# First routing: operands in the ranks' PSUM bank, first one-hots on ScalarE, the leading expert chosen right behind the ranks

## The chip, the cores and the metric

One core of a Trainium2 chip runs the whole kernel. The metric is the device time of one execution in microseconds (us), lower is better. The time before is 495.26 us, the median of 3 runs (494.83 to 495.79).

## What is computed

A linear attention with a normalised output is followed by two mixtures of experts (8 experts, 512 wide, 1024 hidden), each of which sends a token to one expert:

```python
kv = np.einsum('bhsd,bhse->bhde', k, v)
out = np.einsum('bhsd,bhde->bhse', q, kv)           # 4 x 8 x 576 x 64
rms = np.sqrt(np.mean(out * out, axis=-1, keepdims=True) + 1e-06)
x = (out / rms * g_norm)                             # as 2304 tokens x 512
# first mixture: tokens with x @ w_skip > 0 only
e_idx = np.argmax(xc @ w_gate, axis=1)
h = np.maximum(xc[mask] @ w1[e], 0.0)
y[mask] = gate_w[mask, None] * (h @ w2[e]);  out[do_compute] = xc + y
# second mixture: all tokens, at most `capacity` per expert, output gate_w * y
```

## The kernel before

The 2304 tokens are 18 tiles of 128. Tiles 0 to 8 are the first half of the first routing, 9 to 17 the second half (they are routed apart, so that the first half's work begins while attention still runs).

Attention goes batch by batch. `emit_kv` sums the key-value product of the next batch on TensorE (PE) in the PSUM bank `acc`. `emit_kvT` then transposes it into the bank `lg`, and two ScalarE (ACT) copies bring it to the SBUF matrix `kvbd`, which every product of that batch needs. `emit_products` computes one tile's output into `ops` (three buffers of two banks), and `emit_tile` normalises it: ACT squares (`sq`) and copies (`og`), VectorE (DVE) sums (`ss`), takes the reciprocal (`ri`), scales the logits (`lh`) and reduces them into `Lall`; GpSimd (POOL) does the two multiplications of 128 x 512 (`og`, `xr`), and a DMA in SyncE's queue (SP) writes the rows to the DRAM tensor `xcat`. `p1u` is a PSUM pool with a single bank each for the names `lg` and `acc`: a new tile of one name waits until all readers of the former are done.

The first routing of one half has these steps. `onehot_all` (L145) takes the maximum of the 8 logits per token, compares, weighs by expert number, takes the maximum again and compares, which gives the one-hot `oh`. `rank_part` (L167) scans it along the tiles (`C`, L173), lets PE add up ranks in `lg` (L178 to L183), and on DVE turns a rank into a block number `hb` and a row `a` within the block (L200 to L204). The tables are built from `os` and `Bt` (L207, L214) and from nine one-hots `As` of 128 x 128, one per tile (L218). Table matmuls (`As` against `Bt`, L794 and L855) then give for each expert's slots the token that sits in it.

The expert with the most tokens in the first half is the leader: `early1` (L780) counts the tokens in another tile `lg` and calls `lead` (L525), and `slot_reg` loads its number into a register, with which SP loads its weights (L329). `early1_rows` (L790) runs the table matmuls for it, makes the indices `gi` (L271 to L273) and gathers its first 128 rows. The expert runs on them in `EARLY_SEQ`: `t` transposes the rows, `h0` to `h3` are blocks of layer 1, `y0` to `y3` of layer 2, `R` the ranks of the second half, `T` the tables of all tokens, `v` dummy matmuls. Behind `T` DVE sorts the tables by slot, and it counts tokens that found no slot (`nrest`, L319). All engines load that count and branch on it (L372 to L374), and then the remaining experts run.

The order on PE is written out by hand: `ATT_SEQ` has a string for each batch (`t` a tile, `m` its products alone, `p` its rest, `c` a piece of the next batch's key-value product, `T` its transposes, `r` one-hots and scan, `R` ranks, `e` choice of the leader, `E` its table and gather, `w` a weight load). On the other engines a scheduler orders by priorities and dependencies; `behind` adds an order without a wait. `late` (L774) puts the first half's routing at the lowest priority.

Of the kernel before, what the change touches and what calls it, by code (L numbers as in the profile page):

```python
# [47 lines left out]
def moe_kernel(ctx: ExitStack, tc: tile.TileContext, qT, kk, vv, aux, w1a, w2a, w1b, w2b, capacity, out):  # L48
# [118 lines left out]
    def rank_part(st, ohv, i0, i1, ps_pool, tag, base=None, bump=None):  # L167
# [11 lines left out]
        if prev is not None:
            nc.tensor.matmul(R, lhsT=ones, rhs=prev.unsqueeze(2).to_broadcast([128, E, n]), start=False, stop=False)  # L180
        if bump is not None:
            nc.tensor.matmul(R, lhsT=identb, rhs=bump.unsqueeze(2).to_broadcast([128, E, n]), start=False, stop=False)
# [1 line left out]
        if prev is None:
            st["sum"] = C[:, :, n - 1]
        else:
            st["sum"] = rt.tile([128, E], BF16, name=nm("sum"))
            ins = nc.gpsimd.tensor_tensor(out=st["sum"], in0=prev, in1=C[:, :, n - 1], op=ALU.add)
            if m == 1 and bump is not None:
                behind(ins, ahead["gather"])  # L190
        if i1 == NT and m == 1:
            order_experts(st, ps_pool, tag)
# [1231 lines left out]
```

## Time and profile before

| what | us |
|---|---|
| median of the runs (3) | 495.26 |
| lowest, highest | 494.83, 495.79 |
| the profiled execution, its own time | 496.99 |
| its span, first to last instruction | 495.3 |
| TensorE matmuls busy in it | 472.4 (95%) |
| VectorE, ScalarE, GpSimd busy | 303.6, 205.3, 146.5 |

The profile is of one execution, and all times inside it are counted from the start of its span; the kernel's time is 1.69 us more than the span. In a timeline a row is a group of equal instructions that follow one another: the start, the time from the first's start to the last's end, engine, line, operation, output and inputs by the program's names, and the number of instructions. In brackets stand the engine's idle time just before and what ended it. Instructions of one engine overlap by about 0.1 us, so that a row may start before the last one ends.

### The profile page before, as it was taken

How to read it: one execution, taken by the hardware profiler on the slowest of the kernel's cores; microseconds unless marked ns; L12 is line 12 of the kernel's file. 1: busy time of each engine (PE TensorE's matmuls, PEld its weight loads, DVE VectorE, ACT ScalarE, POOL GpSimd, SP SyncE). 2: the span in 40 equal slices, each digit the busy share in tenths (PEclk: the TensorE clock that was granted, in tenths of full speed). 3: DMA queues.
4: the chain of work that ended last, by engine and by line, in shares of the span. 5: the costliest groups of instructions: out<-in, count | busy, mean ns of one | idle time of the engine just before them, and what ended most of it. 6: DMA issues, size and time to landing. Idle time of an engine off the chain costs nothing.

```text
span 495.3 us, 10229 instructions
## 1 busy us (share of the span) xinstructions
PE 472.4 (95%) x3829; PEld 450.1 (91%) x3829; DVE 303.6 (61%) x942; ACT 205.3 (41%) x524; POOL 146.5 (30%) x179
## 2 busy tenths in 40 slices
PE   6998689999999999999998999999999999999995
PEld 3897578999999999999897899999999999999984
DVE  2157988568766775356774576565657566675711
ACT  1376451354352532106143364454545545555400
POOL 5288684104112032022123240220604124040201
PEclk9599999999999999999999999999999999999999
DMA  8999495998868676259119983554656656300001
GB/s 244 367 360 343 166 356 145 359 357 313 293 216 284 228 246 235 97 195 346 60 47 343 396 293 140 201 189 154 212 185 221 204 174 216 148 37 1 36 23 41
DMA packets 24617, 104.90 MB, mean 212 GB/s; under 512 B 3609, under 2 KB 4761, under 8 KB 15984
## 3 DMA queue, kind: packets, MB, share of 16 engines
q1 hardware_dynamic: 17264, 77.75, 45.6%
q0 software_dynamic: 7008, 26.35, 15.2%
q8 instruction: 32, 0.52, 0.4%
q14 instruction: 25, 0.20, 0.1%
q10 hardware_dynamic: 288, 0.07, 0.1%
HBM read 92.15 MB, written 12.76 MB: 212 GB/s over the span
## 4 chain that ended last, share of the span: by engine, by line
PE 75%; DVE 4%; DMA 2%; issue 1%; ACT 0%; POOL 0%; POOLq 0%; ACTq 0%
PE hp L592 14%; PE yp L1086 7%; PE yp L1088 7%; PE yp L1087 7%; PE hp L1086 6%; PE yp L616 6%; PE hp L1087 6%; PE hp L1088 6%; PE yp L626 5%; PE yp L617 2%; PE yt L1317 2%; DMA wraw<-in_w1b 2%; PE tp L1273 2%; PE tp L1010 1%; PE tp L574 1%; DVE wlo L979 1%
## 5 line engine op out<-in xcount | busy, mean ns | idle before, releaser
L978 ACT CAST whi<-wraw 128x512 fp32r<-128x512 f32 x152 | 86.1, 619 | 75.0 <-PE yp L1087 30.1
L979 DVE TENSOR_TENSOR wlo<-wraw,whi 128x512 fp32r<-128x512 f32 x152 | 97.3, 685 | 28.9 <-ACT whi L978 27.8
L339 POOL DMA_INDIRECT rows<-xcat,gi x40 | 42.6, 1064 | 137.3 <-ACT ex L348 86.0
L1086 PE MATMUL hp<-xh,whi 128*128 128x256 f32 (+7 forms) x256 | 78.9, 308 | 0.2 <-DVE hl L1106 0.2
L592 PE MATMUL hp<-xT,wraw 128*128 128x128 f32 (+8 forms) x576 | 78.0, 292 | 0.3 <-issue 0.3
L1088 PE MATMUL hp<-xh,wlo 128*128 128x256 f32 (+7 forms) x256 | 76.6, 299 | 0.0
L1087 PE MATMUL hp<-xl,whi 128*128 128x256 f32 (+7 forms) x256 | 76.6, 299 | 0.0
L592 PEld LDWEIGHTS hp<-xT,wraw 128*128 128x128 f32 x576 | 73.4, 190 | 2.5 <-issue 2.4
L1307 POOL DMA_INDIRECT out<-ot,toki x24 | 34.6, 1444 | 85.4 <-DVE su L352 39.4
L1086 PE MATMUL yp<-hh,whi 128*128 128x320 f32 (+5 forms) x192 | 58.8, 306 | 0.0
L1087 PE MATMUL yp<-hl,whi 128*128 128x320 f32 (+5 forms) x192 | 57.3, 298 | 0.0
L1088 PE MATMUL yp<-hh,wlo 128*128 128x320 f32 (+5 forms) x192 | 57.2, 298 | 0.0
L1086 PEld LDWEIGHTS hp<-xh,whi 128*128 128x128 f32 x256 | 48.2, 188 | 1.0 <-DVE hl L1106 0.7
L1087 PEld LDWEIGHTS hp<-xl,whi 128*128 128x128 f32 x256 | 48.4, 189 | 0.0
L1088 PEld LDWEIGHTS hp<-xh,wlo 128*128 128x128 f32 x256 | 48.2, 188 | 0.0
L1026 POOL DMA_INDIRECT xcat<-rows,toki x16 | 16.4, 1026 | 92.5 <-DVE mxt L297 90.0
L616 PE MATMUL yp<-hT,whi 128*128 128x352 f32 (+4 forms) x160 | 43.1, 351 | 0.0
L1105 ACT ACTIVATE hh<-hp 128x320 fp32r<-128x320 f32 (+8 forms) x64 | 27.2, 429 | 32.2 <-PE hp L1088 27.4
L1106 DVE SCALAR_TENSOR_TENSOR hl<-hp,hh 128x320 fp32r<-128x320 f32 (+8 forms) x64 | 30.1, 477 | 13.5 <-ACT hh L1105 12.3
L617 PE MATMUL yp<-hT,wlo 128*128 128x176 f32 (+4 forms) x160 | 37.8, 236 | 0.0
L1087 PEld LDWEIGHTS yp<-hl,whi 128*128 128x128 f32 x192 | 36.2, 188 | 0.0
L1086 PEld LDWEIGHTS yp<-hh,whi 128*128 128x128 f32 x192 | 36.1, 188 | 0.0
(253 smaller groups left out, 866.6 us busy)
## 6 DMA issues: line engine op xcount, KB each, us to landing
wraw<-in_w1a SPq DMA_DIRECT2D x14, 1024.0 KB
wraw<-in_w2a SPq DMA_DIRECT2D x14, 1024.0 KB
wraw<-in_w1b SPq DMA_DIRECT2D x14, 1024.0 KB
wraw<-in_w2b SPq DMA_DIRECT2D x14, 1024.0 KB
xcat<-xr SPq DMA_DIRECT2D x18, 264.0 KB
q<-in_q SPq DMA_DIRECT2D x3, 1152.0 KB
wraw<-in_k SPq DMA_DIRECT2D x6, 512.0 KB
wraw<-in_v SPq DMA_DIRECT2D x6, 512.0 KB
```

What stands on the lines that cost most here:

```text
L339: return nc.gpsimd.indirect_dma_start(out=rows[:n], out_offset=None, in_=xcat[0:source], in_offset=bass.IndirectOffsetOnAxis(ap=gi[:n], ax ...
L592: nc.tensor.matmul(hp[:, ff, :], lhsT=wv[:, fc % 4, k, :], rhs=XT[j][:, k, c0:c1], start=(k == 0), stop=(k == 3))
L616: nc.tensor.matmul(yp, lhsT=wh[:, fc, :], rhs=HT[j][:, fc], start=(fc == 0), stop=False, skip_group_check=True)
L617: nc.tensor.matmul(yp[:, 0, :], lhsT=wl[:, fc, :], rhs=HT[j][:, fc, 0, :], start=False, stop=(fc == 7), skip_group_check=True)
L978: nc.scalar.copy(out=hi[:, cs], in_=raw[:, cs])
L979: ins = nc.vector.tensor_tensor(out=lo[:, cs], in0=raw[:, cs], in1=hi[:, cs].bitcast(F32), op=ALU.subtract)
L1086: nc.tensor.matmul(ps, lhsT=wh, rhs=xh, start=first, stop=False)
L1087: nc.tensor.matmul(ps, lhsT=wh, rhs=xl, start=False, stop=False)
L1088: nc.tensor.matmul(ps, lhsT=wl, rhs=xh, start=False, stop=last)
L1105: ea = nc.scalar.activation(out=hh[:, fs, cs], in_=hp, func=AF.Relu)
L1106: ev = nc.vector.scalar_tensor_tensor(out=hl[:, fs, cs], in0=hp, scalar=0.0, in1=hh[:, fs, cs].bitcast(F32), op0=ALU.max, op1=ALU.subtract)
L1307: st = nc.gpsimd.indirect_dma_start(out=out, out_offset=bass.IndirectOffsetOnAxis(ap=r2["toki"][:nn, j, bi:bi + 1], axis=0), in_=ot[:nn], ...
```

## The change

The first routing gets functions of its own, `rank_part1` and `lead1`. All steps of a half use one tile `lg` of 512 columns: the ranks, the counts and the short-lived results stand in different columns of one PSUM bank, so that most DVE steps have one operand there and one in SBUF. For the first half the nine one-hots are made on ScalarE, as Relu(1 - (row - a)^2), and the leader is chosen at once behind the tables' right side `Bt`. The sum over both halves (POOL, L188) goes; PE adds the two counts in PSUM. The multiplications of later tiles on POOL all stand behind the gather now. `R` and `T` come earlier among the early expert's blocks.

```diff
-EARLY_SEQ = "v7 t v3 h0 h1 R h2 h3 T y0 y1"
-ATT_SEQ = [..., "r t0 q c0 c1 t1 t2 c2 c3 R c4 t3 T", "e m0 m1 E w w p0 p1 t2 w w t3 t4"]
+EARLY_SEQ = "t v6 h0 R h1 h2 T h3 y0 y1"
+ATT_SEQ = [..., "r t0 q c0 c1 t1 t2 c2 c3 R e w w c4 t3 T", "m0 E m1 p0 p1 t2 w w t3 t4"]
...
-    def onehot_all(dst, c0, i0, i1, chosen, after=None):
+    def onehot_all(dst, c0, i0, i1, chosen, after=None, lg=None):
...
+        if lg is None:
+            mx = rt.tile([128, NT], F32, name="oa_mx")
+            eq = rt.tile([128, NT, E], F32, name="oa_eq")
+        else:
+            mx = lg[:, 80:80 + n]
+            eq = lg[:, 96:96 + n * E].rearrange("p (i e) -> p i e", e=E)
...
+    def rank_part1(st, i0, i1, bump=None):
+        n = i1 - i0
+        lg = p1u.tile([128, 512], F32, name="lg")
+        R, cps = lg[:, 0:E * n].rearrange("p (e i) -> p e i", e=E), lg[:, 72:72 + E]
+        rk, os_ = lg[:, 170:170 + n], lg[:, 180:180 + 4 * n].rearrange("p (i q b) -> p i q b", q=2, b=2)
+        oh = rt.tile([128, E, n], BF16, name=nm("oh1"))
+        onehot_all(oh, 0, i0, i1, ALU.is_gt, lg=lg)
...
+        nc.vector.tensor_tensor_scan(out=C.rearrange("p e i -> p (e i)"), data0=smask[n].rearrange("p e i -> p (e i)"),
+                                     data1=oh.rearrange("p e i -> p (e i)"), initial=0.0, op0=ALU.mult, op1=ALU.add)
+        yield
...
+        if prev is None:
+            counts()
+        nc.tensor.matmul(R, lhsT=ones, rhs=C, start=True, stop=False)
...
+        ranked = nc.vector.tensor_tensor(out=rk8, in0=R, in1=oh, op=ALU.mult)
+        nc.vector.tensor_reduce(out=rk, in_=rk8.rearrange("p e i -> p i e"), axis=AX.X, op=ALU.add)
...
+        sign = -1.0 if prev is not None else 1.0
+        nc.vector.tensor_scalar(out=hb, in0=rk, scalar1=128.0, scalar2=sign * 128.0, op0=ALU.is_ge, op1=ALU.mult)
+        nc.vector.tensor_tensor(out=na, in0=hb, in1=rk, op=ALU.add if prev is not None else ALU.subtract)
+        for k, op in enumerate((ALU.is_lt, ALU.is_ge)):
+            nc.vector.scalar_tensor_tensor(out=os_[:, :, :, k], in0=rk.unsqueeze(2).to_broadcast([128, n, 2]), scalar=128.0,
+                                           in1=pi100[:, i0:i1, :], op0=op, op1=ALU.mult)
+        table_sides(st, oh, os_, i0, 0, n, 4)
+        if prev is None:
+            for i in range(n):
+                nc.scalar.activation(out=As[:, i0 + i], in_=rowb, func=AF.Square, bias=na[:, i:i + 1])
+            nc.scalar.activation(out=As[:, i0:i1], in_=As[:, i0:i1], func=AF.Relu, bias=one1, scale=-1.0)
+            st["lead"] = lead1(lg, cps, ranked)
+        else:
+            for i in range(n):
+                nc.vector.tensor_scalar(out=As[:, i0 + i, :], in0=rowb, scalar1=na[:, i:i + 1], scalar2=None, op0=ALU.is_equal)
+
+    def lead1(lg, cps, after):
+        key, lack, oneP = (lg[:, c:c + E] for c in (220, 228, 236))
+        ins = nc.vector.tensor_tensor(out=key, in0=cps, in1=sev, op=ALU.add)
+        behind(ins, after)
...
+        order = rt.tile([1, 1], I32, name="order_1l")
+        nc.vector.tensor_copy(out=order, in_=of)
...
+        return order, one, bump, head
...
             def early1_rows(n, one):
-                ips = p1u.tile([128, E, 2 * NB1], F32, name="acc")
+                acc = p1u.tile([128, 64], F32, name="acc")
+                ips = acc[:, 0:32].rearrange("p (e x) -> p e x", e=E)
...
+                tab, tok = acc[:, 32:34], acc[:, 34:35]
+                nc.vector.tensor_reduce(out=tab, in_=lt.rearrange("p e q -> p q e"), axis=AX.X, op=ALU.add)
+                nc.vector.tensor_copy(out=r1["tab"][:, 0, :, 0], in_=tab)
+                nc.vector.scalar_tensor_tensor(out=tok, in0=tab[:, 1:2], scalar=128.0, in1=r1["tab"][:, 0, 0, 0:1], op0=ALU.mult, op1=ALU.add)
...
-                if "gather" in ahead and k == 0 and i > ahead["first"]:
+                if "gather" in ahead and k == 0:
                     behind(ins, ahead["gather"])
...
-                        late(lambda: next(gen))
+                        next(gen)
...
-                        warm(p1u.tile([128, 512], F32, name="lg"), int(u[1:]))
+                        warm(p1y.tile([128, 2, 128], F32, name="yp1"), int(u[1:]))
```

The order on three engines around the change follows. A row is a line of the program, the operation, output and inputs, the size and how often it repeats.

ScalarE at the last batch's transposes, before: `sq` and `og` belong to tile 12, and the two `kvbd` copies follow them.

```order
L758 COPY xr<-Lall 128x16 x2
L739 ACTIVATE sq<-ops 128x512
L747 COPY og<-ops 128x512
L713 COPY kvbd_202<-lg 128x4x128
L714 COPY kvbd_202<-acc 128x4x34
L749 ACTIVATE rm<-ss,eps_123 128x8
```

The same place after the change:

```order
L819 COPY xr<-Lall 128x16 x2
L800 ACTIVATE sq<-ops 128x512
L271 ACTIVATE As<-rowb,na_0_771 128x128 x9
L808 COPY og<-ops 128x512
L272 ACTIVATE As<-As,one_123 128x1152
L810 ACTIVATE rm<-ss,eps_125 128x8
L774 COPY kvbd_204<-lg 128x4x128
L819 COPY xr<-Lall 128x16
L775 COPY kvbd_204<-acc 128x4x34
```

The nine Squares, the Relu, a square root and one copy of logits now stand ahead of the second `kvbd` copy.

VectorE from the block numbers of the first half on, after the change (before, the choice of the leader was spread among the one-hots and two tiles' steps):

```order
L263 TENSOR_SCALAR hb_0_770<-lg 128x9
L264 TENSOR_TENSOR na_0_771<-hb_0_770,lg 128x9
L266 SCALAR_TENSOR_TENSOR lg<-lg,pi_88 128x18 x2
L211 TENSOR_TENSOR Bt_207<-oh_0_650,lg 128x288
L802 TENSOR_REDUCE ss<-sq 128x8
L281 TENSOR_TENSOR lg<-lg,sev 128x8
L284 TENSOR_REDUCE mx_1l<-lg 128x1
L286 SCALAR_TENSOR_TENSOR oe_1l<-lg,mx_1l,rowf 1x8
L288 TENSOR_REDUCE lg<-oe_1l 1x1
L290 CAST order_1l<-lg 1x1
```

The leader's number `order_1l` now comes a few short steps behind `Bt`, with one reduction `ss` between.

GpSimd around the gather of the leader's rows, before:

```order
L762 TENSOR_TENSOR og<-og,au 128x512
L762 TENSOR_TENSOR xr<-og,ri 128x512
L762 TENSOR_TENSOR og<-og,au 128x512
L762 TENSOR_TENSOR xr<-og,ri 128x512
L339 DMA rows<-xcat,gi_209 128x528
L762 TENSOR_TENSOR og<-og,au 128x512
L762 TENSOR_TENSOR xr<-og,ri 128x512 x2
```

And after the change:

```order
L823 TENSOR_TENSOR og<-og,au 128x512
L823 TENSOR_TENSOR xr<-og,ri 128x512
L408 DMA rows<-xcat,gi_211 128x528
L823 TENSOR_TENSOR og<-og,au 128x512 x2
L823 TENSOR_TENSOR xr<-og,ri 128x512 x2
L823 TENSOR_TENSOR og<-og,au 128x512
L823 TENSOR_TENSOR xr<-og,ri 128x512
L823 TENSOR_TENSOR og<-og,au 128x512
```

Both multiplications of tile 13 moved from ahead of the gather to behind it.

## Rows read from the trace of the kernel before

**Rows 1.** Stages: us, busy us (instructions) of PE, PEld, DVE, ACT, POOL; PEclk; DMA share; GB/s

```profile
60.00:65.00 5.00, 5.00 (x25) 4.96 (x25) 4.20 (x15) 1.75 (x6) 3.64 (x4) 0.66 0.99 359
...
68.90:82.80 13.90, 12.42 (x117) 11.78 (x114) 11.59 (x53) 4.32 (x11) 5.50 (x9) 1.00 0.59 199
...
82.80:103.00 20.20, 19.93 (x191) 19.69 (x192) 12.88 (x58) 7.74 (x22) 5.50 (x7) 1.00 0.90 313
103.00:240.00 137.00, 137.00 (x1178) 133.33 (x1178) 87.59 (x327) 50.60 (x135) 27.96 (x26) 1.00 0.72 249
```

**Rows 2.** Timeline of TensorE, 50 to 83 us.

```profile
52.76 0.17 PE L783 MATMUL lg<-C,ones 128*128 128x8 bf16 x1 [0.84 <-ACT kvbd L713]
...
59.73 0.35 PE L794 MATMUL acc<-Bt,As 128*128 128x32 bf16 x2 [1.31 <-DVE As L218]
59.94 5.22 PE L730 MATMUL ops<-kvbd,q 128*128 128x162 f32 x24
...
68.41 0.63 PE L574 MATMUL tp<-ident,rows 128*128 128x128 f32 x4 [1.74 <-DMA rows<-xcat,gi]
...
73.20 0.20 PE L183 MATMUL lg<-oh,ntri 128*128 128x72 bf16 x1
...
77.47 0.38 PE L855 MATMUL acc<-Bt,As 128*128 128x32 bf16 x9
...
82.75 3.81 PE L626 MATMUL yp<-hT,wraw 128*128 128x128 f32 x32 [1.16 <-PEq L374]
```

**Rows 3.** Timeline of VectorE, 44 to 82 us.

```profile
44.69 0.97 DVE L157 TENSOR_TENSOR oa_eq<-Lall,oa_mx 128x72 f32<-128x72 f32 x1
45.69 0.96 DVE L158 TENSOR_TENSOR oa_eq<-oa_eq,w 128x72 f32<-128x72 f32 x1
...
46.95 0.23 DVE L160 TENSOR_TENSOR oa_eq<-oa_eq,oa_mx 128x72 f32<-128x72 f32 x1
...
47.73 0.31 DVE L173 TENSOR_TENSOR_SCAN C<-smask,oh 128x72 bf16<-128x72 f32 x1
...
49.23 0.18 DVE L196 TENSOR_TENSOR rk<-lg,oh 128x72 f32<-128x72 f32 x1
...
50.78 1.03 DVE L200 TENSOR_SCALAR hb<-rk 128x9 f32<-128x9 f32 x1
...
53.96 0.26 DVE L207 SCALAR_TENSOR_TENSOR os<-hb,pi 128x18 bf16<-128x18 f32 x2
...
56.39 0.89 DVE L533 TENSOR_SCALAR lead_1l<-key_1l,mx_1l 128x8 f32<-128x8 f32 x1
...
60.87 0.94 DVE L271 SCALAR_TENSOR_TENSOR tok<-tab 128x1 f32<-128x1 f32 x1
...
61.85 0.15 DVE L272 TENSOR_SCALAR gi<-tok 128x1 int32<-128x1 f32 x1
...
68.25 0.38 DVE L757 TENSOR_REDUCE Lall<-lh 128x17 f32<-128x136 f32 x1
...
72.26 0.31 DVE L173 TENSOR_TENSOR_SCAN C<-smask,oh 128x72 bf16<-128x72 f32 x1
...
81.16 0.14 DVE L319 CAST nrest<-nrf 1x1 int32<-1x1 f32 x1
```

**Rows 4.** Timeline of GpSimd, 49 to 63 us.

```profile
49.50 1.28 POOL L762 TENSOR_TENSOR og<-og,au 128x512 f32<-128x512 f32 x1 [0.21 <-ACT og L747]
50.73 2.06 POOL L762 TENSOR_TENSOR xr<-og,ri 128x512 f32<-128x512 f32 x2
...
62.30 1.29 POOL L339 DMA_INDIRECT rows<-xcat,gi  x1 [0.50 <-DVE gi L272]
```

**Rows 5.** Timeline of ScalarE, behind the first routing.

```profile
70.82 0.20 ACT L848 ACTIVATE act<-xT 128x1 f32<-128x1 f32 x1
...
91.39 0.29 ACT L348 ACTIVATE ex<-rows,nx 128x8 f32<-128x8 f32 x1
...
98.96 2.18 ACT L978 CAST whi<-wraw 128x512 fp32r<-128x512 f32 x4 [2.71 <-DMA wraw<-in_w2a]
```

More of the change, by code (lines that the diff above doesn't have):

```diff
@@ L39 @@
 AS_POOL = 0
-WARM_T, LATE = 2, 100000
+WARM_T = 2
 def blocks(n):
@@ L110, in warm @@
         for _ in range(n):
-            nc.tensor.matmul(ps, lhsT=zb[:, 0:128], rhs=zb, start=True, stop=True, skip_group_check=True)
+            nc.tensor.matmul(ps, lhsT=zb[:, 0:128], rhs=zb[:, 0:512 if len(ps.shape) == 2 or ps.shape[1] == 4 else 256], start=True, stop=True, skip_group_check=True)
     act0 = cst.tile([128, 1], F32, name="act0")
@@ L176, in rank_part @@
         R = ps_pool.tile([128, E, n], F32, name=tag)
-        prev = st["sum"]
         nc.tensor.matmul(R, lhsT=ones, rhs=C, start=True, stop=False)
[L179 to L182, printed above, removed]
         nc.tensor.matmul(R, lhsT=ntri, rhs=ohv, start=False, stop=True)
[L184 to L192, printed above, removed]
+        st["sum"] = C[:, :, n - 1]
         rk8 = rt.tile([128, E, n], F32, name=nm("rk8"))
@@ L254, in sort_experts @@
         st["order"] = first(st, EQ[0:1], f"_{m}")
-    def order_experts(st, ps_pool, tag):
-        m = st["m"]
-        cps = ps_pool.tile([128, E], F32, name=tag)
-        nc.tensor.matmul(cps, lhsT=ones, rhs=st["sum"], start=True, stop=True)
-        key = rt.tile([128, E], F32, name=f"key_{m}")
-        nc.vector.tensor_tensor(out=key, in0=cps, in1=st["head"], op=ALU.add)
-        sort_experts(st, key)
-        cnt0 = rt.tile([1, E], F32, name=f"cnt0_{m}")
-        nc.scalar.copy(out=cnt0, in_=cps[0:1])
-        st.update(ends=cnt0)
     def tokens(st, js, ks, empty=T):
@@ L769, in moe_kernel @@
             emit_kvT(0)
-            def late(f):
-                p = tc.cur_priority
-                tc.cur_priority = p + LATE
-                f()
-                tc.cur_priority = p
-            def choose_part(i0, i1, bump=None):
-                oh = choose1(i0, i1)
-                yield from rank_part(r1, oh, i0, i1, p1u, "lg", bump=bump)
-            def early1():
-                cps = p1u.tile([128, E], F32, name="lg")
-                nc.tensor.matmul(cps, lhsT=ones, rhs=r1["sum"], start=True, stop=True)
-                one, bump = lead(cps, 128, "_1l")
-                r1["head"] = rt.tile([128, E], F32, name="head")
-                nc.vector.scalar_tensor_tensor(out=r1["head"], in0=one, scalar=8192.0, in1=sev, op0=ALU.mult, op1=ALU.add)
-                ahead["reg"] = slot_reg(first(r1, one[0:1].unsqueeze(1), "_1l"), 0, False)
+            def early1():
+                order, one, bump, r1["head"] = r1["lead"]
+                ahead["reg"] = slot_reg(order, 0, False)
+                W[0] = []
```

94 lines of the change are left out of this document (66 added, 28 removed).

## The prediction

> **What bounds the kernel now.** I read the busy times by stage first, then the timeline of each engine where TensorE (PE) is not full. From 82.80 us on PE has next to no gap: 19.93 us busy of 20.20, then 137.00 of 137.00 [rows 1]. What starts PE's steady run of expert work earlier by 1 us therefore ends the kernel about 1 us earlier, as long as weights and rows keep up. Before it, from 68.90 to 82.80, PE is busy 12.42 of 13.90 us [rows 1], and before that it waits in several places. So the question is when the last two blocks of expert 0's second layer (the row at 82.75) start [rows 2].
>
> Backwards from there: the 82.75 row waits 1.16 us for a branch on the count of left-over tokens [rows 2], which VectorE (DVE) has only at 81.16 + 0.14 = 81.30 [rows 3]; the branch costs 1.45 us from there. The transposes at 68.41 wait 1.74 us for the gathered rows of the leading expert [rows 2]. The gather's indices are done at 61.85 + 0.15 = 62.00 [rows 3], and its issue on GpSimd (POOL) runs from 62.30 to 63.59 [rows 4]. Ahead of the indices stands the first routing on DVE, stretched: steps of 0.2 us take about 1 us. L157 and L158 take 0.97 and 0.96 where the same shape at L160 takes 0.23; L200 on 9 columns takes 1.03, L533 on 8 columns 0.89, L271 on one column 0.94 [rows 3]. POOL was inside a multiplication of 1.03 us (two in 2.06) [rows 4] when L200 and its followers ran; L200 starts at 50.78, just behind the first one's start at 50.73, and ends with it at 51.8. All slow steps have their tensor inputs in SBUF. L196, of 72 columns with one input in PSUM, takes 0.18 [rows 3] although POOL was busy in that stage too. So the stretch is a wait for POOL, and an operand in PSUM escapes it.
>
> **The change, part by part.** *One operand in PSUM, first half.* L157 and L158 lose 0.97 + 0.96 - 2 x 0.23 = 1.47 us; the scan ends near 46.6 instead of 48.04, and all behind it moves up 1.45 us. From L200 at 50.78 to L207 at 53.96 three steps take 3.18 us [rows 3]; now two steps of some 0.2 us each. The one-hot's argument is ready at 49.33 + 0.4 = 49.7. DVE writing PSUM does not occur before; I take it at the SBUF price, since reading PSUM costs no more (0.18 against 0.23).
>
> *Nine one-hots go to ScalarE (ACT).* The nine on DVE ended so late that PE's last two table matmuls began at 59.73 after 1.31 us of waiting [rows 2]. On ACT they are nine Squares of 128 columns with a bias tile, and one Relu of 1152. No such row exists. Lower end: the activation without bias, 0.20 us for one column, plus 127 columns at the cast's slope; four casts of 512 columns take 2.18, so 0.52 apart, about 1 ns a column [rows 5]. That is 0.3 long and, overlapping by 0.1, some 0.2 apart; a bias-free copy's start-to-start could bring it to 0.17. Upper end: nearly the cast's whole 0.52. I take 0.29 apart, because the row with a bias tile takes 0.29 already for 8 columns [rows 5] and this form has one. Nine make 2.6 us, the output copy between them 0.5 (512 columns, as a cast), the Relu 1.3: from 50.2 to 54.6. This is not beside other work: both copies of the last batch's key-value matrix now stand behind it in ACT's queue, and one waits for a logits copy besides. I get them done at 56.2. Before, PE had them at 52.76 [rows 2]. The transposes that feed them also wait longer, since the bank is in use until the leading expert is chosen (about 52.5), but ACT is later still, so this costs nothing more.
>
> *Products and tables.* PE takes the first product at 56.3, all nine table matmuls right behind it (everything they need is ready at 54.6), at 57.0 to 57.35, against 60.08 at the end of the last two before. Five small DVE steps and one reduction in between bring the indices to 58.8 instead of 61.85: 3.0 us earlier. The last four products follow at 57.35. Twenty-four rows took 5.22 us [rows 2], part of it at a granted clock of 0.66 in that stage [rows 1]; 32 rows, paced by DVE, end near 62.2. Before, the last logits came 3.5 us behind the last product, at 68.63 [rows 3]; now at about 65.9, 2.7 us earlier.
>
> *Gather and POOL.* The gather issues at 59.1 to 60.4, and DMA is emptier then because the first weight loads start when the leader's number is ready, near 52.3. I let the rows land by 63. The transposes then wait for a PSUM bank of the products, to 63.7, and the dummy matmuls for the last product's bank, to 65.4. First-layer block h0 runs from 66.1 to 68.0. The weights' second half is issued behind four row writes; the block that needs it comes at 76, ten microseconds after, so I cost it at nothing; without that cover it would cost up to the load's own time beyond 76.
>
> *Second half of the routing.* From the last logits (68.63) to the end of the scan (72.57) it takes 3.94 us [rows 3]; without the stretch in its three comparisons 2.2: 68.1. But POOL now has all multiplications of the last five tiles behind the gather: four of 1.28 and five of 1.03 [rows 4], and copies, 10.7 us, so until 71. The scan still has two SBUF inputs and meets POOL: + 0.9, 69.0. Ranks end on PE at 69.4. Before, 73.20 + 0.20 to the table matmuls at 77.47 took 4.07 us [rows 2] with POOL nearly idle; now the comparison matrices of the expert sort, both inputs in SBUF, meet its last two multiplications: + 0.9. Tables start at 69.4 + 4.07 + 0.9 = 74.4. PE covers this with h1 and h2 (3.8 us, two blocks as in the row of 3.81 [rows 2]) until 73.2, then idles 1.2.
>
> *New order of blocks.* Tables 0.4, h3 1.9, y0 and y1 3.8: 80.5. The branch needs 82.75 - 77.47 = 5.28 us from the tables' start, 79.7, so its 1.16 us is now hidden by y0 and y1. Removed for nothing: the sum on POOL, a count matmul, four of ten dummy matmuls; these lay in waits.
>
> **Sum.** 80.5 instead of 82.75 is 2.25 us. The profiled execution took 496.99 us, its span 495.30; so 494.74. It was 1.73 above the median of the runs (495.26); on the runs' scale this makes **493.0 us**.
>
> **Rivals.** *A, less contention.* The Squares at 0.17 apart (1.1 us earlier) and no wait for POOL in the second half (1.9): 493.0 - 3.0 = 490.0. For it: DVE may get in between two POOL instructions. Against: in the first half the slow steps came one after the other.
>
> *B, the second half pays it back.* Scan, two comparison matrices, the order's product and the one-hots each wait one whole POOL instruction of 1.03 [rows 4], 5.2 us instead of my 1.8: 493.0 + 3.4 = 496.4 at most, 495.3 with two thirds of it. For it: L157 and L158 each lost 0.74 in a row. Against: POOL's queue is nearly empty by then. [...]
>
> *C, slower: ACT's one-hots hold back the products.* They stand ahead of the copies that PE needs. At 0.52 apart, the upper end, the nine take 4.7 us, 2.1 more, and every microsecond there goes into the products, the logits and the ranks: 495.1. PE then idles through most of 49 to 58; an idle stretch like that (before 59.73) was followed by a granted clock of 0.66 over 60 to 65, a third of 5 us or 1.7 us lost [rows 1]: 496.8. It decides against the change once the copies are later than 56.2 + 2.25 = 58.5. [...] Against C: bias-free rows suggest 0.2.
>
> *D, a PSUM operand doesn't help* (writes to PSUM are slow, or the wait stays): first half as before, choice of the leader and one-hots about 2 us later than I have them: 495.
>
> **How the numbers follow.** Forecast 0.45, A 0.25, B 0.13, C 0.12, D 0.05. The range 489.8 to 495.9 takes in A, most of B, and D, and leaves out C with the clock and the end of B. About 0.2%, 1 us, is what a measurement of this kernel can tell from no change. Faster: forecast and A, 0.70. Within it: most of B, and D, 0.18. Slower: C, 0.12.
>
> **What would show it.** Right: L157, L158 and L200's successors near 0.2 us; nine Squares some 0.3 apart; the last copy of the key-value matrix near 56; index step near 59; a scan of about 1 us in the second half; y2 without a branch wait near 80.5. Wrong: those steps still near 1 us; table matmuls later than 59.7; PE waiting for weights at y0; a low clock in h0 to h3; or PE gaps behind 82 that give the start back.

## The result, and the profile after

The changed kernel takes **498.56 us** (median of 4 runs, 498.18 to 498.94) beside 495.12 us of the kernel before in the same comparison (494.83 to 495.79): a ratio of 1.0068, 95% interval [1.005, 1.0085]. It is slower, where 493.0 was forecast. The profiled execution took 498.52 us, its span 496.9.

The timeline of PE after the change, by the columns of [rows 2], around the first routing and the early expert:

```profile
52.90 0.59 PE L113 MATMUL lg<-zb 128*128 128x512 bf16 x1 [4.11 <-DVE head_1l L298]
53.70 1.06 PE L769 MATMUL lg<-ident,vk 128*128 128x128 f32 x4 [0.22 <-issue]
54.56 1.76 PE L772 MATMUL acc<-gw,vk 128*128 128x34 f32 x8
56.25 3.39 PE L791 MATMUL ops<-kvbd,q 128*64 128x162 f32 x16
59.57 0.39 PE L843 MATMUL acc<-Bt,As 128*128 128x32 bf16 x9
...
73.41 0.22 PE L240 MATMUL lg<-C,ones 128*128 128x72 bf16 x1 [2.72 <-DVE C L228]
...
73.71 5.10 PE L661 MATMUL hp<-xT,wraw 128*128 128x128 f32 x32
78.64 0.38 PE L909 MATMUL acc<-Bt,As 128*128 128x32 bf16 x9
...
80.82 3.76 PE L695 MATMUL yp<-hT,wraw 128*128 128x128 f32 x32
85.40 3.84 PE L695 MATMUL yp<-hT,wraw 128*128 128x128 f32 x32 [0.82 <-ACTq L443]
```

Block y2, the last row, starts at 85.40 and not at 82.75 [rows 2]. PE now stands still in two places where it did not before: 4.11 us ahead of the last batch's transposes, because the bank `lg` is held until VectorE has read it for `head_1l`, the last step of the leader's choice, and 2.72 us ahead of the second half's ranks, because the scan `C` is late. Behind both waits the same work takes longer: the `gw` product (L772) 1.76 us, and h1 and h2 5.10, where e1 below has 0.98 and 3.82. The busy times of these stretches, by the columns of [rows 1]:

```profile
52.80:59.20 6.40, 6.08 (x28) 5.43 (x29) 0.94 (x4) 2.95 (x7) 2.32 (x2) 0.50 0.81 295
...
72.90:76.30 3.40, 2.89 (x18) 2.89 (x18) 2.87 (x19) 0.00 (x0) 0.64 (x3) 0.51 1.02 388
...
103.00:240.00 137.00, 137.00 (x1192) 133.33 (x1191) 85.81 (x321) 51.00 (x136) 27.87 (x26) 1.00 0.74 255
```

PEclk is 0.50 and 0.51 behind the two waits. From 103 on, at 1.00, PE is as full as before [rows 1], so what the start lost stays lost.

VectorE in the same execution, by the columns of [rows 3]:

```profile
44.51 0.23 DVE L163 TENSOR_TENSOR lg<-Lall,lg 128x72 f32<-128x72 f32 x1
44.78 0.24 DVE L164 TENSOR_TENSOR lg<-lg,w 128x72 f32<-128x72 f32 x1
...
49.31 0.16 DVE L263 TENSOR_SCALAR hb<-lg 128x9 f32<-128x9 f32 x1
49.50 0.17 DVE L264 TENSOR_TENSOR na<-hb,lg 128x9 f32<-128x9 f32 x1
...
52.69 0.15 DVE L298 SCALAR_TENSOR_TENSOR head_1l<-lg,sev 128x8 f32<-128x8 f32 x1
...
61.34 0.16 DVE L851 TENSOR_SCALAR gi<-acc 128x1 int32<-128x1 f32 x1
...
68.17 0.66 DVE L818 TENSOR_REDUCE Lall<-lh 128x17 f32<-128x136 f32 x2
...
70.73 2.63 DVE L228 TENSOR_TENSOR_SCAN C<-smask,oh 128x72 bf16<-128x72 f32 x1
...
82.34 0.14 DVE L388 CAST nrest<-nrf 1x1 int32<-1x1 f32 x1
```

The steps with an operand in PSUM take what was forecast, 0.16 to 0.24 us instead of about 1 [rows 3], and L163 and L164 (44.51 to 45.02) take it inside GpSimd's two multiplications from 44.35 to 46.41. The scan of the second half takes 2.63 us, where the same shape took 0.31 [rows 3]. GpSimd at that time, and ScalarE's one-hots, in their timelines:

```profile
69.79 1.26 POOL L823 TENSOR_TENSOR og<-og,au 128x512 f32<-128x512 f32 x1
71.02 1.03 POOL L823 TENSOR_TENSOR xr<-og,ri 128x512 f32<-128x512 f32 x1
72.00 0.19 POOL L819 COPY xr<-Lall 128x16 f32<-128x16 f32 x1
72.16 1.03 POOL L823 TENSOR_TENSOR xr<-og,ri 128x512 f32<-128x512 f32 x1
73.15 0.20 POOL L819 COPY xr<-Lall 128x16 f32<-128x16 f32 x1
```

```profile
50.15 2.72 ACT L271 ACTIVATE As<-rowb,na 128x128 bf16<-128x128 bf16 x9
...
53.24 1.26 ACT L272 ACTIVATE As<-As,one 128x1152 bf16<-128x1152 bf16 x1
...
56.35 0.27 ACT L775 COPY kvbd<-acc 128x136 f32<-128x136 f32 x1 [0.30 <-PE acc L772]
```

The scan ends at 73.36, together with five GpSimd instructions that follow one another without a gap (73.15 + 0.20 = 73.35). ScalarE did as forecast: (2.72 - 0.39) / 8 = 0.29 us apart (0.39 is a single one, from e4_kvt_ops), and the last `kvbd` copy ends at 56.62, beside 56.2 in the forecast. But what that copy waited for was PE's `gw` product (the bracket of the row at 56.35), not ScalarE's own queue.

### The profile page after: what moved, and what is told of

Same layout as the page of the kernel before. It is cut to its first block, busy times and chain, and to the rows that moved or that the text cites. A ratio compares the mean times of both kernels' runs of the same rounds, so it can differ in the third digit from the quotient of the medians.

```text
span 496.9 us, 10223 instructions
## 1 busy us (share of the span) xinstructions
PE 472.2 (95%) x3822; PEld 451.8 (91%) x3826; DVE 298.3 (60%) x935; ACT 208.8 (42%) x533; POOL 145.5 (29%) x178
## 4 chain that ended last, share of the span: by engine, by line
PE 76%; DVE 3%; DMA 2%; ACT 0%; issue 0%; POOL 0%; POOLq 0%; ACTq 0%
PE hp L661 14%; PE yp L1140 7%; PE yp L1142 7%; PE yp L1141 7%; PE hp L1140 7%; PE hp L1141 6%; PE hp L1142 6%; PE yp L685 6%; PE yp L695 5%; PE yp L686 2%; PE tp L1327 2%; DMA wraw<-in_w1b 2%; PE yt L1371 2%; PE tp L1064 1%; PE tp L643 1%; PE lg L1051 1%
## 5 line engine op out<-in xcount | busy, mean ns | idle before, releaser
L661 PE MATMUL hp<-xT,wraw 128*128 128x128 f32 (+8 forms) x576 | 79.5, 295 | 0.3 <-ACT xT L645 0.3
L661 PEld LDWEIGHTS hp<-xT,wraw 128*128 128x128 f32 x576 | 74.7, 193 | 2.4 <-issue 1.8
```

Of the source, the lines that this page charges most:

```text
L661: nc.tensor.matmul(hp[:, ff, :], lhsT=wv[:, fc % 4, k, :], rhs=XT[j][:, k, c0:c1], start=(k == 0), stop=(k == 3))
```

## The experiments

Theory 1: the loss is the wait for the bank `lg` and the low clock behind it. Theory 2: it is the scan's wait for GpSimd, which the new order exposes. Rivals: ScalarE's queue, the new order of blocks, and PSUM operands as such. Kernels of one group ran on the same chip, and each ratio is to the kernel before in those runs. Its median was 495.78 beside e1 to e4, 496.76 beside e5 to e8, 496.51 beside e10 to e13 and 495.70 beside e14, e9 and e15, so a difference between the medians of two groups can be off by a microsecond or more; the ratios and the ruler below are the safer measure. Single executions also differ at the start of attention, so the table has a ruler beside the time: how long it takes from PE's last row of 32 matmuls `acc<-wraw` (behind it come the first half's ranks) to y2, both from PE's timeline of the one profiled execution, which took 501.04 us in e2 and 499.77 in e14, above their medians. "Repair" stands for each of the two edits that e3 and e4 make.

| kernel | `acc<-wraw` | y2 | between | median us | ratio to before |
|---|---|---|---|---|---|
| before | 45.14 | 82.75 | 37.61 | 495.12 | 1 |
| changed | 44.97 | 85.40 | 40.43 | 498.56 | 1.0068 [1.005, 1.0085] |
| e1_fill_bank_wait | 44.97 | 81.00 | 36.03 | 494.29 | 0.9982 [0.996, 1.0005] |
| e2_fill_scan_wait | 46.37 | 84.99 | 38.62 | 497.01 | 1.0033 [1.0005, 1.0062] |
| e3_scan_psum | 45.54 | 82.94 | 37.40 | 495.62 | 0.9993 [0.9973, 1.0012] |
| e4_kvt_ops | 45.63 | 80.11 | 34.48 | 492.36 | 0.9936 [0.9919, 0.9952] |
| e5_as_dve | 46.01 | 86.84 | 40.83 | 499.78 | 1.0091 [1.0059, 1.0122] |
| e6_pool_order | 45.09 | 83.91 | 38.82 | 496.08 | 0.9995 [0.9969, 1.0021] |
| e7_psum_onehots_only | 45.90 | 88.23 | 42.33 | 499.22 | 1.0066 [1.004, 1.0092] |
| e8_seq | 45.77 | 83.49 | 37.72 | 495.85 | 0.9978 [0.9947, 1.001] |
| e10_kvt_m1 | 45.58 | 82.53 | 36.95 | 495.65 | 0.9985 [0.9962, 1.0008] |
| e11_kvt_m1_scan | 44.04 | 78.13 | 34.09 | 492.11 | 0.9904 [0.9868, 0.994] |
| e12_kvt_asdve | 45.52 | 83.05 | 37.53 | 497.29 | 0.9988 [0.9955, 1.0021] |
| e13_psum_first_half | 45.54 | 82.07 | 36.53 | 494.03 | 0.9932 [0.9905, 0.9958] |
| e14, the changed kernel again | 46.41 | 88.13 | 41.72 | 497.91 | 1.0041 [1.0027, 1.0055] |
| e9_kvt_scan | 44.65 | 78.91 | 34.26 | 491.36 | 0.9928 [0.99, 0.9956] |
| e15, as e11 | 45.19 | 79.24 | 34.05 | 491.37 | 0.9923 [0.99, 0.9946] |

### The bank and the clock: e1 and e4

e1 leaves the wait where it is and fills it with 18 dummy matmuls in the other bank, so that what changes there is the clock:

```diff
+            if b == B - 1:
+                warm(p1u.tile([128, 512], F32, name="acc"), 18)
             tp = p1u.tile([128, 4, 128], F32, name="lg")
```

> The change with 18 dummy matmuls of 512 columns in the bank acc, ahead of the last batch's transposes, where TensorE waits 4.11 us for the bank lg. Theory clock (the wait lowers the granted clock, and the transposes and products behind it run at 0.50): the clock stays 1.00 from 52 to 59, the table matmuls of the first half start near 57.2 instead of 59.57, and the time falls by 2 to 2.5 us, to about 496.3. Theory queue (the key-value copies are late behind ScalarE's one-hots, the clock matters little): the table matmuls stay later than 59, the time stays at 498.5.

PE's timeline of e1, and two of its stretches:

```profile
48.75 4.04 PE L113 MATMUL acc<-zb 128*128 128x512 bf16 x17
...
53.24 0.60 PE L771 MATMUL lg<-ident,vk 128*128 128x128 f32 x4
...
56.54 0.39 PE L845 MATMUL acc<-Bt,As 128*128 128x32 bf16 x9
...
70.38 0.19 PE L240 MATMUL lg<-C,ones 128*128 128x72 bf16 x1 [0.78 <-DVE C L228]
...
70.57 3.82 PE L661 MATMUL hp<-xT,wraw 128*128 128x128 f32 x32
```

```profile
48.70:52.80 4.10, 3.99 (x17) 1.76 (x18) 3.72 (x19) 3.64 (x13) 2.51 (x3) 1.00 1.00 349
52.80:59.20 6.40, 6.38 (x56) 5.79 (x55) 2.91 (x13) 4.87 (x11) 2.74 (x3) 1.00 0.87 314
```

The transposes start within half a microsecond of the changed kernel's, 53.24 and 53.70, but at a clock of 1.00 instead of 0.50, and the time falls by 498.56 - 494.29 = 4.3 us to what the kernel before takes. The gain splits by the rows: 0.46 at the transposes; from there to the leader's indices 58.31 - 53.24 = 5.07 instead of 61.34 - 53.70 = 7.64, which is 2.57; from the indices to the ranks 12.07 in both; from the ranks to y2 10.62 instead of 11.99, which is 1.37 and mostly the price of the slow blocks h1 and h2 (3.82 and 5.10). Together 4.4, twice the 2 to 2.5 us that I expected: the last 1.37 does not come from the dummies' own place. In e1 block h0 ran slow (2.74 us instead of 1.95, PEclk 0.69 from 66 to 70 us), and the wait behind it was 0.78 instead of 2.72. With that said, the low clock (0.50) alone costs as much as the whole loss.

e4 takes the wait itself away: the last batch's transposes and the `gw` product go into a buffer of `ops`, and its two dummy matmuls are left out.

```diff
-            tp = p1u.tile([128, 4, 128], F32, name="lg")
-            warm(tp, WARM_T)
+            both_ = apo.tile([128, 4, 256], F32, name="ops") if b == B - 1 else None
...
+                tp = both_[:, :, 0:128]
...
-            wp = p1u.tile([128, 4, 128], F32, name="acc")
+            wp = p1u.tile([128, 4, 128], F32, name="acc") if both_ is None else both_[:, :, 128:256]
```

> The change with the last batch's transposes in a buffer of the products instead of the bank lg (its two dummy matmuls go). Theory bank (TensorE waits for lg until the leader is chosen; everything late in the first half comes from it): the transposes start near 48.8 instead of 53.70, the key-value copies end near 51, the table matmuls start behind the Relu near 55 instead of 59.57, indices near 56.5 instead of 61.34, the clock holds; the second half moves up by 3 to 4 us and the time with it, to about 495. Theory ScalarE (its one-hots hold the copies back in any case): the copies stay behind 54, and less than 1 us is won.

PE's timeline of e4:

```profile
49.50 0.66 PE L773 MATMUL ops<-ident,vk 128*128 128x128 f32 x4
...
55.87 0.39 PE L847 MATMUL acc<-Bt,As 128*128 128x32 bf16 x9 [2.64 <-ACT As L272]
...
69.28 0.19 PE L240 MATMUL lg<-C,ones 128*128 128x72 bf16 x1 [0.64 <-DVE C L228]
```

The transposes come at 49.50, and what holds PE next is the step that the prediction had feared, ScalarE's one-hots, for 2.64 us. 492.36 us is 6.2 below the changed kernel, and the interval [0.9919, 0.9952] puts it below the kernel before. Two things came along with the repair. The scheduler put the two `kvbd` copies ahead of eight of the nine Squares (51.11 and 51.57 in ScalarE's timeline), so that they no longer stand behind the one-hots; e1 left them there and still won the loss back. And the indices came at 58.10, not near 56.5, while the time fell 3 us further than I expected; part of that is luck with the scan, which took 0.77 us here. Theory 1 stands, on e1 above all.

### The scan and GpSimd: e2, e3, e6 and e8

e2 fills PE's wait for the scan with dummies: `"t v6 h0 v24 R h1 h2 T h3 y0 y1"`.

> The change with 24 dummy matmuls of 256 columns between h0 and R, where TensorE waits 2.72 us for the scan. Theory clock: the granted clock stays 1.00 from 73 to 76, h1 and h2 take 3.8 instead of 5.1 us, the tables start 1.0 us earlier (then they wait for VectorE's one-hots, done at 77.5), the time falls by about 1 us, to 497.5. Theory scan (only the late ranks matter, the clock is made up behind them): no change, 498.5.

h1 and h2 take 3.82 instead of 5.10 us; the scan, 2.64, and the wait for the bank stay. On the ruler this is worth 1.81 us, and 498.56 - 497.01 = 1.55 in the time. e3 puts the scan's mask into PSUM and so leaves the scan one SBUF input:

```diff
+        sm1 = lg[:, 256:256 + E * n]
+        nc.vector.memset(sm1, 1.0)
+        nc.vector.memset(sm1.rearrange("p (e i) -> p e i", e=E)[:, :, 0:1], 0.0)
...
-        nc.vector.tensor_tensor_scan(out=C.rearrange("p e i -> p (e i)"), data0=smask[n].rearrange("p e i -> p (e i)"),
+        nc.vector.tensor_tensor_scan(out=C.rearrange("p e i -> p (e i)"), data0=sm1,
```

> The change with the scan's mask in the PSUM bank (two memsets more per half). Theory scan (it waits 2.2 us for GpSimd's multiplications because both its inputs lie in SBUF): it takes 0.3 to 0.5 us instead of 2.63, the ranks start near 71.5 instead of 73.41, the clock does not fall behind it, y2 starts near 82.5 instead of 85.4, and the time falls by 2.5 to 3.3 us, to about 495.5. If the comparison matrices of the sort then meet GpSimd instead, half of it: 497. Rival (the scan waits for something else, such as the copy of the one-hots): no change, 498.5.

VectorE's timeline of e3, behind the last logits:

```profile
70.76 0.31 DVE L231 TENSOR_TENSOR_SCAN C<-lg,oh 128x72 bf16<-128x72 f32 x1
...
71.70 1.43 DVE L330 TENSOR_TENSOR G<-key 128x64 f32<-128x64 f32 x1
```

GpSimd's instructions follow one another without a gap from 69.64 to 73.04 in its timeline, and the scan takes 0.31. But one multiplication ends at 70.89, while the scan runs, so e3 alone does not show that the operand in PSUM freed it. e9, which has the same mask (below), does: its scan lies wholly inside one multiplication, and so does that of e11 (65.75 to 66.06).

```profile
67.26 0.31 DVE L231 TENSOR_TENSOR_SCAN C<-lg,oh 128x72 bf16<-128x72 f32 x1
```

```profile
66.84 1.04 POOL L830 TENSOR_TENSOR xr<-og,ri 128x512 f32<-128x512 f32 x1
```

In e3 the ranks come 71.12 - 45.54 = 25.58 us behind the ruler's start instead of 73.41 - 44.97 = 28.44, which is 2.86 earlier, and y2 3.03 earlier. `G`, with both inputs in SBUF, now waits in the scan's place, but beside PE's h1 and h2. Theory 2 stands beside theory 1.

e6 moves GpSimd's two multiplications of tile 13 back ahead of the gather:

```diff
-                if "gather" in ahead and k == 0:
+                if "gather" in ahead and k == 0 and i > ahead["first"]:
...
+                        ahead.setdefault("first", t[int(u[1])])
```

> GpSimd's two multiplications of tile 13 stand ahead of the gather again, as in the kernel before. Theory 2 (the scan of the second half waits for the whole train of GpSimd multiplications behind it): GpSimd is through 2 us earlier, the scan at 70.73 takes 0.3 to 1.3 instead of 2.63, ranks 1 to 2 us earlier; the gather issues up to 1 us later, which the dummy matmuls and the wait for the last products cover. Time 496 to 497.5. Rival (the scan's length does not come from GpSimd's queue but from its place, or the gather's delay costs as much as the scan gains): 498 to 499.5.

VectorE's and then GpSimd's timeline of e6:

```profile
71.49 0.31 DVE L228 TENSOR_TENSOR_SCAN C<-smask,oh 128x72 bf16<-128x72 f32 x1
```

```profile
70.58 1.04 POOL L823 TENSOR_TENSOR xr<-og,ri 128x512 f32<-128x512 f32 x1
71.57 0.22 POOL L819 COPY xr<-Lall 128x16 f32<-128x16 f32 x1
```

The time is inside what was expected of theory 2, but not by the reason given: GpSimd is through hardly earlier (its last multiplication ends at 72.79 there, at 73.19 in the changed kernel). The scan arrived just as one multiplication ended (71.49 and 71.62), and it took 0.31 with GpSimd's next ones behind it. So a scan with both inputs in SBUF can be short too. The place in GpSimd's train where it arrives does not settle its length: in e1 and e4 it arrived 0.27 and 0.44 us into the same multiplication (67.98 and 68.02 in GpSimd's timelines) and took 2.08 and 0.77.

e8 puts h1 ahead of the ranks and T behind h3: `"t v6 h0 h1 R h2 h3 T y0 y1"`.

> The changed kernel with blocks h0 and h1 ahead of the second half's ranks R, as before the change, and the tables T behind h3: t v6 h0 h1 R h2 h3 T y0 y1. Theory 2 (PE's wait of 2.72 us for the scan and the low clock in h1 and h2, about 1.3 us, are the price of the new order): both go, h0 and h1 take 3.8 together, PE reaches y0 2.5 to 3.5 us earlier than 80.82, but the tables come at 77 to 78, so the count is late and the branch waits 1 to 2 us ahead of y2: 496 to 497.5. Rival (the new order is right, and the second half's lateness comes from the first half alone): no change, 498 to 499.

The scan still takes 2.63, PE waits 0.94 for it instead of 2.72, and h0 to h3 all run at 3.74 to 3.82 for two. 495.85 is better than expected of theory 2. With a late scan the new order costs about 2.7 us, by the medians and on the ruler.

### ScalarE's one-hots: e5 and e12

e5 gives the nine one-hots back to VectorE, in the program behind the leader's choice.

> The nine one-hots of the first half go back to VectorE, behind the choice of the leader; nothing else changes. Theory 1 (the transposes' wait for the bank lg, held until the leader's one-hot head_1l is read, and the low clock behind it): the wait of 4.1 us at 52.90 stays, since VectorE chooses the leader at the same time, the clock is still 0.50 from about 53 to 59, and the time stays within 1.5 us of the changed kernel's 498.56: 497 to 500. Rival (ScalarE's queue: Squares and Relu ahead of the kvbd copies hold the products back): the copies come 2 to 3 us earlier, table matmuls near 57 instead of 59.57, and the time falls to 495 to 496.

The scheduler placed the one-hots among the leader's steps, and PE waited for the bank even longer, 5.71 us instead of 4.11, again until VectorE had read it for `head_1l`. The 499.78 us lie inside theory 1's 497 to 500. So ScalarE's queue was not what held the transposes back, but e5 changes the wait too and says little on where the one-hots belong. e12 says more on that: the same edit with the transposes in `ops`.

> The last batch's transposes in an ops buffer, and the nine one-hots on VectorE instead of ScalarE. Theory (ScalarE's one-hots are a gain once the bank does not hold up the transposes: they end at 55.8 there, and on VectorE nine of them compete with the logits' steps and the leader's choice): indices at 59 to 60.5 instead of 58.1, time 0.5 to 2.5 us above e4: ratio 0.995 to 0.999. Rival (ScalarE's 2.64 us wait was the loss): ratio 0.990 to 0.993.

The ratio came as expected of the theory, 0.9988, while a step of its reason did not: the indices were ready at 57.63, earlier than e4's 58.10. What suffers is the logits of the later tiles on VectorE; PE waits 1.80 us there for `lh`, 2.16 for the next one, and y2 waits 2.02 at the branch. The ruler reads 37.53 against 34.48, which is 3.05 more: 2.10 of it up to the ranks (25.75 against 23.65), the rest in the wait ahead of y2, which nothing here ties to the one-hots. By the ratios it is 0.9988 - 0.9936 of the time, 2.6 us, with intervals that do not overlap but on two chips, and e12's executions scatter (492.2 to 498.54). So with the bank repaired ScalarE's one-hots are worth some 2 to 3 us.

### The PSUM operands alone: e7 and e13

Both are the kernel before with only the short-lived operands of `onehot_all` in a tile of the bank `lg`, e7 for both halves, e13 for the first (the call in e13; inside `onehot_all` the operands move as in the change):

```diff
-            onehot_all(oh, 0, i0, i1, ALU.is_gt)
+            onehot_all(oh, 0, i0, i1, ALU.is_gt, lg=p1u.tile([128, 512], F32, name="lg") if i0 == 0 else None)
```

> The kernel before, with the short-lived operands of the one-hot steps alone (maximum, comparison, weighing) in a PSUM tile of the bank lg, for both halves. Theory: the prediction's step on L157 and L158 holds: both near 0.23, the first half's one-hot 1.4 us earlier, and no new wait for the bank, since the ranks use it behind the one-hots anyway; in the second half 1 to 1.5 us earlier as well, but hidden there by blocks h0 and h1. The table matmuls of the leader (59.73 before) move up 0 to 1.4 us: 494 to 495.5, no more than 1.5 us below the kernel before. Rival (any use of bank lg by the routing steps delays the transposes and their clock): 496 to 498.

> The kernel before with the one-hot steps of the first half alone in a PSUM tile; the second half keeps SBUF, so the dummy matmuls v7 of the bank lg do not wait for it (in e7_psum_onehots_only they waited 4.88 us). Theory: the steps at L157 and L158 take near 0.23, and nothing holds the bank longer: 494 to 495.5 on the scale of 495.26, ratio 0.996 to 1.000. Rival (a PSUM operand there delays another reader of the bank, or the order of VectorE's steps shifts for the worse): ratio 1.002 or more.

e7 went against my theory, and its 499.22 us lie above the rival's range as well. The steps take 0.22 to 0.24 us in both halves, and the transposes are not held up (49.97, ahead of the table matmuls at 55.38). The wait is for the same bank in another place:

```profile
70.27 3.14 PE L111 MATMUL lg<-zb 128*128 128x512 bf16 x7 [4.88 <-DVE oh L162]
```

The dummies `v7` ahead of the gathered rows use `lg` there, and the second half's one-hot holds it until its last read. (The change moved these dummies to another bank, and left the transposes in this one.) e13, without that wait, is faster than the kernel before: L157 and L158 take 0.23 and 0.24, the indices come 60.94 - 45.54 = 15.40 us behind the ruler's start instead of 61.85 - 45.14 = 16.71, 1.31 earlier, and y2 1.08 earlier. The ratio, 0.9932, lies below the 0.996 to 1.000 that I expected; the ruler's 1.08 us, 0.998 of the time, lies inside it, and the kernel before scattered in those runs (493.78 to 501.2). The PSUM operands are a gain, and the bank that they share is a loss.

### Both repairs together: e10, e11, e14, e9, e15

e10 is e4 with `"m0 m1 E"` for `"m0 E m1"`, e11 adds e3's mask. e9 has both repairs and no other order; e14 and e15 repeat the changed kernel and e11 beside it.

> The changed kernel with the last batch's transposes in an ops buffer (as in e4_kvt_ops) and the products of the second tile ahead of the leader's table matmuls: m0 m1 E instead of m0 E m1. Theory (PE's wait of 2.64 us for ScalarE's one-hots and the clock of 0.50 behind it still cost 2 to 3 us there): the eight product matmuls fill part of the wait, the clock falls later or not at all, the table matmuls stay near 55.9, and the time falls by 0.5 to 2 us below e4's 492.36, ratio 0.989 to 0.9925. Rival (what follows is paced by VectorE's steps on the logits, so a fuller PE there gives nothing): ratio as in e4, 0.9925 to 0.995.

> As e10_kvt_m1, and the scan's mask in PSUM (as in e3_scan_psum). Theory: the two repairs act on different waits, but the scan's was only 0.77 us long once the transposes were repaired, so this adds 0.3 to 1 us: ratio 0.987 to 0.992. Rival (the sort of the tables then meets GpSimd's last multiplications and gives it back): same as e10 within 0.3 us.

> The changed kernel itself once more, on the same chip as the next two. Expected: the ratio of 1.0068 [1.005, 1.0085] again, between 1.002 and 1.009, with PE's wait of 4.1 us for the bank lg and the scan of 2.6 us in the profile.

> The changed kernel with both repairs and no other order: the last batch's transposes in an ops buffer (as e4_kvt_ops), the scan's mask in PSUM (as e3_scan_psum). Theory 1 (these two waits, with the clock behind them, are the whole loss): 5.5 to 7 us below the changed kernel in the same runs, ratio to the kernel before 0.990 to 0.994, no more than 0.5 us from e11_kvt_m1_scan. Rival (the earlier products m1 are needed as well, against the 2.64 us wait for ScalarE's one-hots): at least 1 us above e11_kvt_m1_scan, ratio 0.9935 or more.

> e11_kvt_m1_scan again, beside e9_kvt_scan on the same chip: ratio 0.987 to 0.993. The start of block y2, counted from the last piece of the key-value product (34.1 us in e11_kvt_m1_scan, 34.5 in e4_kvt_ops), stays within 0.3 us of 34.1.

e10 missed: the 2.64 us wait shrank to 1.34, but the scan met GpSimd's train again, and the clock fell behind PE's wait (0.70 from 70.30 to 76.00). Its scan on VectorE, and PE's rows behind it:

```profile
67.50 2.74 DVE L228 TENSOR_TENSOR_SCAN C<-smask,oh 128x72 bf16<-128x72 f32 x1
```

```profile
70.30 0.19 PE L240 MATMUL lg<-C,ones 128*128 128x72 bf16 x1 [2.44 <-DVE C L228]
...
70.48 5.44 PE L661 MATMUL hp<-xT,wraw 128*128 128x128 f32 x32
```

e4 had escaped this by luck (its scan took 0.77). With the mask in PSUM the ruler falls from 36.95 to 34.09, more than the 0.3 to 1 us that I expected, since I had taken e4's scan for e10's. e14 repeats the slowdown, at a ratio of 1.0041 and with the same waits (4.11 and 2.73 us, the scan 2.63). e9 beside e14 and e15 then settles it: 491.36 us, 497.91 - 491.36 = 6.55 below the changed kernel, and equal to e15 (491.37). The two waits, with what follows them, are more than the whole loss, and the earlier products add nothing beyond 0.2 us on the ruler. e4 is below the kernel before with one repair fewer, but with the lucky scan; e9 does not need that luck. It is 495.70 - 491.36 = 4.3 us below the kernel before, more than the 2.25 that the prediction had for the change. PE's next waits in it are 2.64 us ahead of the table matmuls, for ScalarE's one-hots, and this one:

```profile
64.55 0.63 PE L646 MATMUL tp<-ident,rows 128*128 128x128 f32 x4 [3.31 <-DMA rows<-xcat,gi]
```

It ends with the landing of the gathered rows, whose indices were ready at 56.91.

## Why the prediction was wrong

**Right: the prices on VectorE and ScalarE.** L157 and L158 near 0.23 (0.23 and 0.24), L200's successors near 0.2 (0.16 and 0.17), writing PSUM at the SBUF price (L163 0.23, beside 0.23 for L160 of the same shape [rows 3]), Squares 0.29 apart, the Relu 1.26 for 1.3. e13 shows that the first term, 1.45 us, passes almost whole to the indices (1.31). Two things were right by luck. The copies were done at 56.62 for 56.2, but the forecast had them late by ScalarE's queue, and they were late by PE's `gw` product, which took 1.76 us at a clock of 0.50 and ended at 56.32; in e1, at 1.00, it took 0.98 and ended at 54.66. And L196 was read as a step that escapes while GpSimd is busy; GpSimd stood idle for 0.21 us just then, up to 49.50 (in its timeline of the kernel before). The steps that do show the escape are L163 and L164 of the changed kernel.

**The step that failed: "the bank is in use until the leading expert is chosen (about 52.5), but ACT is later still, so this costs nothing more".** The date was right (52.69 + 0.15 = 52.84), and "ACT is later still" held too (the Relu, which stands ahead of the copies, ends at 53.24 + 1.26 = 54.50). As a matter of waiting alone the bank cost 0.9 us at most (the indices come 58.31 - 44.97 = 13.34 us behind the ruler's start in e1, 58.10 - 45.63 = 12.47 in e4, where the copies had moved up in ScalarE's queue besides). But I compared only the dates of two inputs and did not ask what PE does meanwhile. It does nothing for 4.11 us, and then runs the transposes, the `gw` product and the first products at a clock of 0.50. Table matmuls came at 59.57 and not at 57.0, the indices at 61.34 and not at 58.8. In e1, at a clock of 1.00, they came at 58.31: the sum up to there was right but for the clock. I had this loss and its price in rival C (a granted clock of 0.66 behind an idle stretch), and tied it to ScalarE's queue at 0.52 apart, which did not happen; it needed only the bank. The chance of 0.12 was on the right outcome with the wrong trigger.

**The second step: "The scan still has two SBUF inputs and meets POOL: + 0.9".** It met five instructions of GpSimd, not one: 2.63 against 0.31, + 2.3; behind PE's wait of 2.72 us for it the clock was low once more (0.51), + 1.3 in h1 and h2. Rival B had whole instructions lost in each of several steps; it was one step that lost several. The comparison matrices that I priced at + 0.9 lost nothing in the changed kernel (`G` took 0.22 at 74.09), since GpSimd was through by then (73.29 + 0.25 = 73.54).

**The third, smaller: the branch "is now hidden by y0 and y1".** The count is known at 82.34, 2.2 us before y1 ends (80.82 + 3.76 = 84.58), and PE still waits 0.82 for the branch; in e4 and e9 the count comes 2.25 us before y1's end too (77.04 against 79.29, 75.84 against 78.09), and the wait is 0.82 again. So this last part of the wait did not hang on the count. ScalarE's timeline shows what goes with it:

```profile
84.62 0.37 ACT L697 COPY yT<-yp 128x256 f32<-128x256 f32 x1 [3.30 <-PE yp L695]
```

This copy of the output of y0 and y1 is ScalarE's last work ahead of the branch, and y2 starts 85.40 - 84.62 = 0.78 us behind its start. In the timelines of PE y2 starts 0.81 or 0.82 us behind y1's end in the changed kernel, e1 to e5, e9, e14 and e15, but 1.19 in e6, 0.93 in e10 and 2.10 in e12 (83.05 and 80.95), so y1's end does not settle it. The brackets of these rows name ScalarE at the branch as what ended PE's wait, those of e5 and e11 the copy itself. The prediction left it out; that PE waits for it is read from these rows, and no run was made to move it.

**The balance.** y2 came 85.40 - 80.5 = 4.9 us later than forecast: the last logits 2.9 (68.83 for 65.9), from there to the ranks 1.1 (4.58 for 3.5: the scan + 1.4 more than I had, and 0.3 less from its end to the ranks), from the ranks to the tables 0.2 (5.23 for 4.97), from the tables to y2 0.7 (6.76 for 6.1). From y2 to the end of the span it took 411.5 us, and 412.55 in the execution profiled before. So of its excess of 1.73 us over the median, which I had taken off, 1.05 is found there, and the other 0.7 is the rest of the miss (4.9 + 0.7 = 5.6). Two slips in the sums changed nothing: 62.2 + 3.5 is 65.7 and not 65.9, and rival A takes 1.9 off for two waits that the sum has at 0.9 each.

## What to carry to other kernels

When short-lived results move into a PSUM bank, list every later user of that bank on TensorE, and when the last reader lets it go: here the saved microsecond on VectorE came with a wait of 4.11 on PE, and dummies in the wrong bank waited 4.88 in e7. A wait of TensorE that lies ahead of late inputs is not free: price the work behind it at a lower clock as a risk (0.50 and 0.51 behind the two waits here; 1.00 behind e9's wait of 3.31 us), and test that with dummies in the wait before repairing anything. And when a step loses its neighbours' cover (the ranks moved one block earlier), look at the longest wait that its input can have, not at the usual one.

## What the runs showed of the hardware

**The clock.** Behind 4.11 us without a matmul PEclk was 0.50 over the next 6.4 us; with dummies in that wait it was 1.00 over the same stretch (e1). Behind 2.72 us it was 0.51 over 3.4; in e14, the same program, h1 and h2 took 6.65 us behind a wait of 2.73, instead of 5.10. Not every such wait did this: behind the 3.31 us in e9 PEclk was 1.00 (65.00 to 72.90), and what made the difference was not tried. In the changed kernel the first wait was one for a PSUM bank and the second one for the scan; e9's was one for a DMA.

**VectorE beside GpSimd.** A scan with both inputs in SBUF took 2.63 us, to the end of five GpSimd instructions, in the changed kernel, and 2.08 to 2.74 in e1, e2, e5, e8, e10 and e14; with one input in PSUM it took 0.31 inside a GpSimd multiplication (e9, e11). The scan is not alone in this: `G`, an operation on two SBUF inputs of 64 columns, took 0.22 in the changed kernel, with GpSimd through, 1.43 and 1.74 in e3 and e11, across two multiplications, and 0.91 in e9, to the end of one. Other steps got in between two GpSimd instructions. VectorE and GpSimd in e13:

```profile
49.88 1.02 DVE L201 TENSOR_SCALAR hb<-rk 128x9 f32<-128x9 f32 x1
50.93 0.96 DVE L203 SCALAR_TENSOR_TENSOR hb<-rk,hb 128x9 f32<-128x9 f32 x1
51.93 1.19 DVE L205 SCALAR_TENSOR_TENSOR a<-hb,rk 128x9 f32<-128x9 f32 x1
```

```profile
49.83 2.04 POOL L763 TENSOR_TENSOR xr<-og,ri 128x512 f32<-128x512 f32 x2
51.83 1.27 POOL L763 TENSOR_TENSOR og<-og,au 128x512 f32<-128x512 f32 x1
```

Each step ends with one instruction of GpSimd (50.90, 51.89, 53.12), and the next step gets its turn. In e4 the scan got its turn after one multiplication (to 69.06) and a copy (69.22): it took 0.77, to 69.23. The three steps in e13 waited for one instruction each, the scan of the changed kernel through five, and what decides whether a waiting step gets in between two GpSimd instructions is open.
